# Closing block of a decode kernel: SyncE clears its own six semaphores while its store flies, GpSimd's wait for the store's issue goes

## The chip, the cores and the metric

The kernel runs on one core of a Trainium2 chip. Times are device microseconds of that core. Two lengths must be kept apart. The **span** goes from the first to the last of the kernel's own instructions. The **measured time** is longer: it also holds what runs behind the kernel's last instruction, called the runtime's part here (its semaphore updates go on in the trace of the kernel before from 130.621 to 132.072 us, 1.79 us past the last instruction at 130.283). ("Time less span" below is the plain difference of the two lengths; what lies behind the span's end is 0.29 us more.)

## The reference

One decode step: a query of one token attends to the last 4096 of 32768 cached keys with 32 heads over 16 cached ones, and beside it a dense layer with gelu runs on the same token; a gate mixes the two.

```python
g = _sigmoid((x * gate_w).sum(-1, keepdims=True))
a = _A_ref(x, A_k_cache, A_v_cache, A_wq, A_wo)    # q = x wq; softmax(q k) v; wo
b = _B_ref(x, B_w1, B_b1, B_w2, B_b2)              # gelu(x w1 + b1) w2 + b2
return g * a + (1 - g) * b                         # 1 x 1 x 576, bf16
```

## The kernel before

It streams 53.6 MB of weights and caches and ends with two copies, one store and a closing block:

```python
    out_row = const.tile([1, D], BF16, name="out_row")
    nc.scalar.copy(out=out_row[:, DH:D], in_=y_out[1])
    nc.vector.tensor_copy(out=out_row[:, 0:DH], in_=y_out[0])
    nc.sync.dma_start(out=out.rearrange("a b d -> (a b) d"), in_=out_row[:])
```

The closing block is written by hand over the one that the framework makes. Its semaphores have numbers 99 to 110: 99 is raised by GpSimd's own instructions, 105 by VectorE, 106 by TensorE, 108 by ScalarE, the others by loads, 110 by the store. Number 96 is the gather count of the block.

```python
    def store_ends_program(nc):
        ...
        last = copy.replace(
            leave, sync_info=mybir.SyncInfo(on_wait=[landed], on_update=[taken])
        )
        kept = [arrive, last]          # SyncE: a DRAIN raises the gather count; wait for the landing
        for engine in (
            mybir.EngineType.Activation,
            mybir.EngineType.PE,
            mybir.EngineType.DVE,
        ):                             # one DRAIN each raises the gather count
            kept.append(next(i for i in end.instructions if i.engine == engine))
        ours = [i for i in end.instructions if i.engine == pool]
        others = mybir.SyncInfo(on_wait=waits, on_update=[])
        kept += [copy.replace(ours[0], sync_info=others), ours[1]]   # GpSimd: all waits, then gather >= 4
        reset, clear, spare, spare2 = ours[3:7]
        lo, hi = reset.reset_range_start, reset.reset_range_stop
        for n, (a, b) in enumerate(((lo, sem), (sem + 1, hi))):
            ...                        # GpSimd: DRAIN and range clear of 99..109, then of an empty range
        end.instructions = kept
```

GpSimd may clear only when SyncE has issued the store, since the store's issue waits for the semaphores of VectorE and ScalarE (in the trace of the kernel before they are raised at 129.070 and 129.046 us, the store's issue starts at 129.122, the clears write from 129.903). That is what the gather count of four is for.

## Time and profile before

| | before |
|---|---|
| time, median of runs | 132.34 us (132.31 to 132.40) |
| span | 130.28 us |
| time less span, mean of 11 runs in one set | 1.98 us, single runs scatter by 0.03 |
| last arithmetic ends | 129.06 us |
| store issued / landed | 129.12 / 130.25 us |

How to read it: the page's busy shares say little here, because semaphore instructions are not counted as busy. The prediction below shows the lines that matter: the closing line in the view of one line of code (kind of instruction, count, duration in ns as min/median/max, first and last start), and the waits of SyncE's queue. The records of semaphore updates are in the same trace. The records of single waits in that trace last 17 to 51 ns and do not hold the waiting: SyncE's wait for the landing is one of 17 ns behind 0.6 us without a record. A record of two waits can hold some: GpSimd's on 107/105 lasts 1682 ns.

### The profile page before, as it was taken

What the parts mean: (1) busy time and instruction counts of PE and PEld (TensorE: products, weight loads), DVE (VectorE), ACT (ScalarE), POOL (GpSimd) and SP (SyncE); (2) the same over time, 40 slices, a digit from 0 to 9 for tenths busy, and PEclk for the clock granted to TensorE, in tenths of its full rate; (3) what the DMA queues carried; (4) which work ended last, traced back from release to release, by engine and by line L of the source; (5) the groups of instructions that cost most, each with busy time, mean ns of one, the idle gap of its engine ahead of it and who ended that gap; (6) DMA issues with size and microseconds to landing.
All of it is one profiled execution on the core that took longest, in us unless ns stands there. A gap on an engine that the chain in (4) does not pass through costs nothing.

```text
span 130.3 us, 2411 instructions
## 1 busy us (share of the span) xinstructions
PE 80.7 (62%) x1145; PEld 46.1 (35%) x1077; DVE 53.7 (41%) x49; ACT 8.3 (6%) x18; POOL 10.1 (8%) x34
## 2 busy tenths in 40 slices
PE   0036999476003998949909995985300930899973
PEld 0036949475000121202201121685300920864641
DVE  0056100300079969999999995604000020010001
ACT  3000000003000000030003003021000000000001
POOL 5029930000000000000000000000000000000000
PEclk9999999999999999999996899975555555555999
DMA  7999999899999899899999999899999999999980
GB/s 232 421 436 439 468 401 498 363 463 438 392 448 463 372 453 483 372 443 473 392 433 463 412 412 463 376 444 473 397 423 448 423 407 421 430 427 421 403 354 25
DMA packets 2508, 53.75 MB, mean 413 GB/s; under 512 B 286, under 2 KB 290, under 8 KB 580
## 3 DMA queue, kind: packets, MB, share of 16 engines
q1 hardware_dynamic: 2490, 53.61, 96.5%
q8 instruction: 8, 0.13, 0.4%
q10 hardware_dynamic: 10, 0.01, 0.0%
HBM read 53.62 MB, written 0.00 MB: 412 GB/s over the span
## 4 chain that ended last, share of the span: by engine, by line
DMA 52%; DVE 24%; PE 14%; issue 6%; SPq 2%
DMA k_t<-in_A_k_cache_dram 27%; DMA w_t<-in_B_w_dram 25%; DVE kt L494 19%; PE s_ps L516 7%; PE o_ps L603 5%; DVE m L532 3%; DVE pt L565 2%; PE y_ps L359 1%; SPq L651 1%; DVE mr L535 1%; SPq L658 0%; SPq L194 0%; PE mt_ps L541 0%; DVE out_row L702 0%; SPq L190 0%
## 5 line engine op out<-in xcount | busy, mean ns | idle before, releaser
L516 PE MATMUL s_ps<-kt,qz_flat 128*128 128x512 bf16 x128 | 32.6, 412 | 17.2 <-DVE kt L494 10.4
L494 DVE STREAM_TRANSPOSE kt<-k_t 128x4096 f32<-128x4096 f32 x8 | 35.3, 4432 | 11.7 <-DMA k_t<-in_A_k_cache_dram 10.3
L603 PE MATMUL o_ps<-pt,v_t 128*128 128x8 bf16 x512 | 14.2, 167 | 16.8 <-DMA v_t<-in_A_v_cache_dram 14.8
L516 PEld LDWEIGHTS <-qz_flat 128*128 128x128 bf16 x64 | 6.8, 107 | 40.3 <-issue 40.2
L603 PEld LDWEIGHTS <-v_t 128*128 128x128 bf16 x512 | 14.1, 102 | 17.5 <-DMA v_t<-in_A_v_cache_dram 15.1
L387 PEld LDWEIGHTS <-w_t 128*128 128x128 bf16 x162 | 10.2, 165 | 0.9 <-issue 0.9
L387 PE MATMUL h_ps<-x,w_t 128*128 128x2 bf16 x162 | 10.4, 202 | 0.0
L359 PE MATMUL y_ps<-w_t,gt 128*1 128x288 bf16 x72 | 7.2, 363 | 1.2 <-DMA w_t<-in_B_w_dram 1.2
L553 ACT ACTIVATE p_t<-s_ps,negm 128x1024 bf16<-128x1024 f32 x4 | 4.5, 1113 | 50.9 <-DVE negm L549 50.9
L633 DVE RECIPROCAL rg<-mt_ps 128x32 f32<-128x32 f32 x1 | 0.4, 358 | 15.5 <-PE mt_ps L628 15.5
L565 DVE STREAM_TRANSPOSE pt<-p_t 128x1024 bf16<-128x1024 bf16 x4 | 4.9, 1224 | 2.7 <-ACT p_t L553 2.7
L425 PE MATMUL q_ps<-x,wq_t 128*128 128x2 bf16 x144 | 4.0, 166 | 2.7 <-DMA wq_t<-in_A_wq_dram 2.7
L702 DVE CAST out_row<-y_ps 1x288 bf16<-1x288 f32 x1 | 0.4, 445 | 11.7 <-PE y_ps L359 11.7
L308 PE MATMUL xs_ps<-one_b,rows 1*128 1x1 bf16 x9 | 0.7, 195 | 7.4 <-DVE rows L302 7.4
L532 DVE TENSOR_REDUCE m<-s_ps 128x1 f32<-128x1024 f32 x4 | 4.8, 1196 | 1.1 <-PE s_ps L516 1.1
L359 PEld LDWEIGHTS <-gt 128*1 128x1 bf16 x72 | 3.7, 99 | 3.6 <-issue 1.6
L425 PEld LDWEIGHTS <-wq_t 128*128 128x128 bf16 x144 | 3.9, 104 | 2.8 <-DMA wq_t<-in_A_wq_dram 2.8
L396 DVE COPY hacc<-h_ps 128x36 f32<-128x36 f32 x1 | 0.2, 196 | 10.6 <-PE h_ps L387 10.6
L359 PE MATMUL y_ps<-wo_t,ov 128*1 128x288 bf16 x62 | 4.3, 286 | 0.2 <-DMA wo_t<-in_A_wo_dram 0.2
L661 DVE TENSOR_TENSOR om<-o_ps,rgh 128x128 bf16<-128x128 f32 x1 | 0.3, 292 | 8.8 <-PE o_ps L603 8.8
L302 DVE COPY rows<-rows 1x1152 bf16<-1x1152 bf16 x1 | 0.7, 748 | 6.5 <-DMA rows<-in_A_x_dram 6.5
L359 PEld LDWEIGHTS <-ov 128*1 128x1 bf16 x62 | 2.6, 83 | 1.8 <-issue 0.8
(77 smaller groups left out, 39.1 us busy)
## 6 DMA issues: line engine op xcount, KB each, us to landing
k_t<-in_A_k_cache_dram SPq DMA_DIRECT2D x4, 4096.0 KB, 31.8
v_t<-in_A_v_cache_dram SPq DMA_DIRECT2D x4, 4096.0 KB, 23.2
wq_t<-in_A_wq_dram SPq DMA_DIRECT2D x1, 4608.0 KB, 25.8
w_t<-in_B_w_dram SPq DMA_DIRECT2D x1, 2880.0 KB, 14.2
w_t<-in_B_w_dram SPq DMA_DIRECT2D x1, 2592.0 KB, 23.1
w_t<-in_B_w_dram SPq DMA_DIRECT2D x1, 2304.0 KB, 8.1
wo_t<-in_A_wo_dram SPq DMA_DIRECT2D x1, 2304.0 KB
wo_t<-in_A_wo_dram SPq DMA_DIRECT2D x1, 2160.0 KB
```

What stands on the lines that cost most here:

```text
L302: nc.vector.tensor_copy(out=xdup.rearrange("p (d t) -> p d t", t=2), in_=x_row.rearrange("p (d o) -> p d o", o=1).to_broadcast([1, D, 2]),)
L359: last = nc.tensor.matmul(y_out[s], lhsT=vec, rhs=row[:, s * DH : (s + 1) * DH], start=start, stop=stop, skip_group_check=True,)
L387: nc.tensor.matmul(h_ps[:, j:NF:NJ], lhsT=w1_t[:, i, j:FH:NJ], rhs=x2[:, i, :], start=False, stop=(i == NI - 1 and j == NJ - 1), skip_grou ...
L425: nc.tensor.matmul(q_ps[:, j : Hq : Hq // 2], lhsT=wq_t[:, i, j * Dh : (j + 1) * Dh], rhs=x2[:, i, :], start=(i == 0 and j == 0), stop=(i ...
L494: lambda: nc.vector.transpose(out=kt[g, f][:].bitcast(FP32), in_=keys.rearrange("p c d -> p (c d)").bitcast(FP32),),
L516: last = nc.tensor.matmul(s_ps[g][:, u * 512 : (u + 1) * 512].rearrange("p (c k) -> p c k", k=32), lhsT=qz(g, j, 2 * f + half), rhs=kv[:, ...
L532: queue("dve", lambda: nc.vector.reduce_max(out=m1[:], in_=s_ps[g][:], axis=AX.X))
L535: lambda: nc.vector.tensor_scalar(out=mr[:], in0=hi16[:], scalar1=m1[:, 0:1], scalar2=None, op0=ALU.mult),
L553: nc.scalar.activation(out=p_t[:].rearrange("p c k -> p (c k)"), in_=s_ps[g][:], func=ACT.Exp, bias=negm[:, 0:1], scale=SCALE, accum_out=s ...
L565: lambda: nc.vector.transpose(out=pt[:, g, :, :].rearrange("p c q -> p (c q)"), in_=p_t[:].rearrange("p c k -> p (c k)"),),
L603: last = nc.tensor.matmul(o_ps[:, 8 * g : 8 * g + 8, 0], lhsT=v_t[g][:, c, :], rhs=pt[:, g, c % 32, 8 * (c // 32) : 8 * (c // 32) + 8], st ...
L651: nc.sync.dma_start(out=wo_t[:, r0:r1, :].rearrange("p r n -> p (r n)"), in_=wo_src[:, 0 : 4 * RW, :].rearrange("h (a r) n -> h a (r n)", ...
```

## The change

The intent: GpSimd shall not wait for the store's issue. For that, the semaphores that SyncE still needs are no longer GpSimd's to clear; SyncE subtracts them itself, one instruction each, while the store flies.

```diff
-        landed = next(w for w in waits if w.id == sem)
-        waits.remove(landed)
-        last = copy.replace(
-            leave, sync_info=mybir.SyncInfo(on_wait=[landed], on_update=[taken])
-        )
-        kept = [arrive, last]
+        first = min(w.id for w in store.sync_info.on_wait)
+        mine = [w for w in waits if w.id >= first and w.id != sem]
+        # ... and TensorE's total, and last the store's own semaphore
+        waits = [w for w in waits if w.id < first]
+        kept = []
+        for w, name in zip(mine, names):
+            # taken: "sem-sub-imm" of w.wait_value
+            kept.append(copy.replace(leave, name=name,
+                sync_info=mybir.SyncInfo(on_wait=[w], on_update=[taken])))
...
-        kept += [copy.replace(ours[0], sync_info=others), ours[1]]
+        three = mybir.SyncInfo(
+            on_wait=[copy.replace(came.on_wait[0], wait_value=3)],
+            on_update=[copy.replace(came.on_update[0], update_value=3)],
+        )
+        kept += [copy.replace(ours[0], sync_info=others), copy.replace(ours[1], sync_info=three)]
-        for n, (a, b) in enumerate(((lo, sem), (sem + 1, hi))):
+        for n, (a, b) in enumerate(((lo, first), (stop, hi))):
```

As built: SyncE has six semaphore instructions (108, 105, 107, 109, 106, 110 in this order) and no DRAIN; GpSimd waits for three, has two waits fewer (those on 107/105 and 109/108), and clears 99 to 104.

More of the change, by code (lines that the diff above doesn't have):

```diff
@@ L119, in store_ends_program @@
         sem = store.sync_info.on_update[0].id
+        act = mybir.EngineType.Activation
+        names = [i.name for i in end.instructions if i.engine == sp]
+        names += [i.name for i in end.instructions if i.engine == act][1:]
         drain, arrive, leave = [i for i in end.instructions if i.engine == sp][:3]
         waits = list(drain.sync_info.on_wait)
-        landed = next(w for w in waits if w.id == sem)
-        waits.remove(landed)
-        taken = mybir.SyncUpdate(
-            sync_type="semaphore",
-            id=sem,
-            ant_name=landed.ant_name,
-            update_mode="sem-sub-imm",
-            update_value=landed.wait_value,
-            update_reg=None,
-        )
@@ L132, in store_ends_program @@
-        last = copy.replace(
-            leave, sync_info=mybir.SyncInfo(on_wait=[landed], on_update=[taken])
-        )
-        kept = [arrive, last]
+        pe = [
+            u
+            for i in body.instructions
+            if i.engine == mybir.EngineType.PE and i.sync_info
+            for u in i.sync_info.on_update
+        ]
+        first = min(w.id for w in store.sync_info.on_wait)
+        mine = [w for w in waits if w.id >= first and w.id != sem]
+        mine.append(
+            copy.replace(
+                mine[0],
+                id=pe[0].id,
+                ant_name=pe[0].ant_name,
+                wait_value=sum(u.update_value for u in pe),
+            )
+        )
@@ new lines, in store_ends_program @@
+        mine.append(next(w for w in waits if w.id == sem))
+        stop = max(w.id for w in mine) + 1
+        assert sorted(w.id for w in mine) == list(range(first, stop))
+        waits = [w for w in waits if w.id < first]
+        own = [i for i in body.instructions if i.engine == sp and i.sync_info]
+        last_wait = max(
+            n for n, i in enumerate(own) if any(w.id < first for w in i.sync_info.on_wait)
+        )
+        last_load = max(
+            n for n, i in enumerate(own) if any(u.id < first for u in i.sync_info.on_update)
+        )
@@ new lines, in store_ends_program @@
+        assert last_wait <= last_load
+        assert len(names) >= len(mine)
+        kept = []
+        for w, name in zip(mine, names):
+            taken = mybir.SyncUpdate(
+                sync_type="semaphore",
+                id=w.id,
+                ant_name=w.ant_name,
+                update_mode="sem-sub-imm",
+                update_value=w.wait_value,
+                update_reg=None,
+            )
+            kept.append(
+                copy.replace(
+                    leave,
+                    name=name,
+                    sync_info=mybir.SyncInfo(on_wait=[w], on_update=[taken]),
+                )
+            )
@@ L143, in store_ends_program @@
         others = mybir.SyncInfo(on_wait=waits, on_update=[])
-        kept += [copy.replace(ours[0], sync_info=others), ours[1]]
+        came = ours[1].sync_info
+        three = mybir.SyncInfo(
+            on_wait=[copy.replace(came.on_wait[0], wait_value=3)],
+            on_update=[copy.replace(came.on_update[0], update_value=3)],
+        )
+        kept += [copy.replace(ours[0], sync_info=others), copy.replace(ours[1], sync_info=three)]
         reset, clear, spare, spare2 = ours[3:7]
         lo, hi = reset.reset_range_start, reset.reset_range_stop
-        for n, (a, b) in enumerate(((lo, sem), (sem + 1, hi))):
+        for n, (a, b) in enumerate(((lo, first), (stop, hi))):
             raw = list(clear.instr)
```

## The prediction

To read it: in the trace of the kernel before, semaphore 2 is raised nine times, five blocks of semaphores are written, and semaphore 2 is raised nine times again. The author takes each nine raises for a barrier of the five engines, a "serpentine" (through the engines and back).

> **What bounds the kernel now.** I read the page first, then the timeline of the last microsecond, then the view of the closing block's line with the waits of SyncE's queue, and last the trace's own list of semaphore updates, because the closing block hardly shows anywhere else. The page:
>
> ```profile
> span 130.3 us, 2411 instructions
> DMA 52%; DVE 24%; PE 14%; issue 6%; SPq 2%
> ```
>
> For most of the span the loads set the pace; the change touches none of that. The timeline from 127 us on:
>
> ```profile
> start us, us, engine line op out<-in xcount [idle before <-releaser]
> 128.62 0.45 DVE L702 CAST out_row<-y_ps 1x288 bf16<-1x288 f32 x1 [11.72 <-PE y_ps L359]
> 128.65 0.39 ACT L701 CAST out_row<-y_ps 1x288 bf16<-1x288 f32 x1 [11.56 <-PE y_ps L359]
> 129.12 0.28 SPq L703 DMA_DIRECT2D out_dram<-out_row  x1
> ```
>
> The last arithmetic ends at 129.06 us, the store's issue runs from 129.12 to 129.40, and yet the span ends at 130.28 and the measured time is 132.34. So 3 us of the measured time lie behind the last computation, and 2 us of them behind the span. The change acts only there. Its line (L729 of the old kernel) in the view of one line, where the columns are duration in ns (min/median/max) and first and last start:
>
> ```profile
> L729 POOLq EVENT_SEMAPHORE  x6: 17/43/1682, 116.8 to 129.7; - x6
> L729 POOLq DRAIN  x3: 26/51/77, 129.2 to 130.0; - x3
> L729 POOLq EVENT_SEMAPHORE_RANGE_CLEAR  x2: 33/64/95, 129.9 to 130.1; - x2
> L729 PEldq DRAIN  x1: 543/543/543, 128.1 to 128.1; - x1
> L729 DVEq DRAIN  x1: 477/477/477, 128.6 to 128.6; - x1
> L729 ACTq DRAIN  x1: 419/419/419, 128.7 to 128.7; - x1
> L729 SPq DRAIN  x1: 207/207/207, 129.5 to 129.5; - x1
> L729 SPq EVENT_SEMAPHORE  x1: 17/17/17, 130.3 to 130.3; - x1
> ```
>
> And the waits of SyncE's queue:
>
> ```profile
> SPq L703 <- DVE out_row L702: 27.6, 1, 27.6
> SPq L729 <- SPq L729: 0.6, 1, 0.6
> ```
>
> The reader is to see two tails. SyncE: store issued, a DRAIN of 207 ns that raises the gather count, then 0.6 us of waiting for the store to land, then one semaphore instruction of 17 ns. GpSimd: waits for the other engines, then DRAIN, clear, DRAIN, clear. The records with all digits, with the semaphore updates of the same trace (numbers as built: 96 gather, 110 the store's, 2 not the kernel's):
>
> ```
> 128.671 129.081 129.116 129.671  sem 96 raised by PE, ACT, DVE, SyncE
> 129.562 130.249                  sem 110 raised (store issued; store landed)
> 129.696-129.713                  GpSimd's wait for four on sem 96
> 130.061-130.094                  GpSimd's second range clear, its last instruction
> 130.266-130.283                  SyncE's wait for the landing, its last instruction
> 128.903 129.231 130.621 130.666 130.689 130.786 130.826 130.860 130.906   sem 2
> 131.715 131.749 131.787 131.831 131.855 131.953 131.991 132.026 132.072   sem 2
> ```
>
> [...] semaphore 2 is raised nine times, resets of five blocks of about 51 follow (7-53, 54-104, 105-155, 156-206, 207-255, 130.82 to 131.63 us), then nine again, 357 ns from first to last. [...]
>
> **Who gates the end.** In the second serpentine nothing is late, and its hops are 34, 38, 44, 24, 98, 38, 35, 46 ns. In the first, hops 4 to 9 are 45, 23, 97, 40, 34, 46: ordinary. So the third arrival, at 130.621, is the late one, and the fourth and fifth engines were already waiting. Which engine is third? The blocks of the reset carry a signature: GpSimd's own clear inside the kernel writes groups of four, 21.7 ns apart (129.903, 129.925, 129.946); block 105-155, the third, is written in groups of four 21.8 ns apart, the others at 30, 17.5, 24 and 6.6 ns. So I take the third for GpSimd, the first for PE (the only one done before 128.903), the last for SyncE. GpSimd's last instruction ends at 130.094, 0.19 us before SyncE's, but it needs 130.621 - 130.094 = 0.527 us to arrive; PE needed 128.903 - 128.658 = 0.245 and ACT at most 129.231 - 129.072 = 0.159. **So GpSimd, whose end looks earlier in the span, sets the end of the program.**
>
> **The change part by part.**
> - *GpSimd's wait.* It now waits for three (PE, ACT, DVE): the last raise is at 129.116 instead of 129.671, 0.555 us earlier. The two double waits on semaphores now SyncE's (107/105 and 109/108) go, so it stands at the gather wait long before. The steps after it are the same five: old spacing from the end of that wait to the end of the last clear is 130.094 - 129.713 = 0.381 us. With the old reaction of 129.713 - 129.671 = 0.042: 129.116 + 0.042 + 0.381 = 129.54. Arrival at the barrier with the same 0.527: 130.07, before 130.62.
> - *SyncE.* Its DRAIN of 207 ns goes; five waits with a subtraction come, all already satisfied, before the sixth, which waits for the landing as before. The one such record on SyncE in the opening (0.716, next instruction 0.794) gives 78 ns apiece: 5 x 78 = 0.39 us, from 129.46 to 129.85. The landing is at 130.249: hidden with 0.40 us to spare. The last instruction still ends at 130.283, so **the span hardly moves** (130.28).
> - *The barrier.* Its fifth arrival becomes SyncE's own: 130.283 plus its tail x. The trace only bounds x: SyncE arrived no later than its turn, so x is under 130.689 - 130.283 = 0.406. The tails seen are 0.159 and 0.245 on two engines and 0.527 on GpSimd. I choose x = 0.22, near the first two, as an estimate: arrival at 130.50 in place of 130.689, **0.19 us saved**. Everything behind (four hops, resets, second barrier) moves with it unchanged.
> - *Sum:* 132.34 - 0.19 = 132.15 us. Of GpSimd's 0.555 us, two thirds are not paid out, because the store's flight takes over as the bound.
>
> **The rivals.**
> 1. *SyncE's tail is as long as GpSimd's was allowed to hide, x near 0.38.* Then only 0.02 us is saved: 132.32. For it: GpSimd's tail of 0.527 shows that tails differ. Against it: PE and ACT.
> 2. *The third arrival is SyncE's (130.283 + 0.338), not GpSimd's.* Then the change takes away what was hidden anyway: 132.34. Against it: the signature of the reset, and that block 207-255 would have to be another's.
> 3. *The five subtractions cost far more than 78 ns, or hold the store up.* They'd have to cost 0.16 us each to reach the landing; at 0.25 each the end would be 0.4 us later, 132.5 at most with what is saved. Against it: SyncE's records of this kind last 17 to 28 ns.
> 4. *A short x, 0.12:* 0.29 us saved, 132.05; the next floor is GpSimd at 130.07, with SyncE's turn at 130.13, out of reach.
>
> **Range and chances.** The first steps (GpSimd free, SyncE hidden) I hold at 8 in 10 or more; the size hangs on x alone, between 0.12 and 0.4. Rivals 1 and 2 set the upper end at 132.34, rival 4 the lower, with some hundredths for the spread of runs (132.33 to 132.40 before): 132.02 to 132.34. Two per cent are 2.6 us; all that lies behind the last computation is 3 us, and most of it is the runtime's or the store's. Hence 0.99 for within 2% and 0.005 on each side.
>
> **What would show it right or wrong.** Right: no DRAIN on SyncE in the closing line, six semaphore instructions on it, five between 129.4 and 130.0 and one near 130.3; GpSimd's clears near 129.3 and 129.5; a span of 130.3 as before; a third raise of semaphore 2 near 130.07 and the fifth near 130.5, with a gap before the fifth and not the third. The third still near 130.6 would mean that it isn't GpSimd's or that its 0.527 us is no constant; the sixth SyncE instruction well after 130.3 would mean that the subtractions or the store's flight grew; the fifth near 130.69 would mean rival 1. A time change without a shift of these marks would be noise.

The forecast's sum: 132.34 - 0.19 = 132.15 us, the 0.19 from 130.689 (the fifth raise), 130.283 (SyncE's end) and the estimate x = 0.22. The "17 to 28 ns" of rival 3 leave out two of SyncE's records in that trace, of 363 and 27544 ns.

## The result, and the profile after

The changed kernel takes 131.76 us (median; 131.71 to 131.95), the kernel before 132.34 in the same rounds. The ratio is 0.9959, with a 95% interval of 0.9941 to 0.9976. Ratios here are the mean time of one kernel's runs over that of the other's of the same rounds, so not quite the ratio of the medians. The change is within 2%, as predicted, but the gain is 0.58 us by the medians in place of 0.19, and the median lies below the predicted range.

The page of the changed kernel, first line and the chain's shares by engine:

```profile
span 130.3 us, 2413 instructions
DMA 52%; DVE 24%; PE 13%; issue 6%; SPq 2%
```

Span and chain are as before: whatever was gained was gained behind the span. The timeline of the last microseconds:

```profile
128.62 0.45 DVE L742 CAST out_row<-y_ps 1x288 bf16<-1x288 f32 x1 [11.72 <-PE y_ps L399]
129.13 0.28 SPq L743 DMA_DIRECT2D out_dram<-out_row  x1
```

The closing line, and the wait of SyncE's queue in it:

```profile
L769 SPq EVENT_SEMAPHORE  x6: 17/17/17, 129.5 to 130.3; - x6
L769 POOLq EVENT_SEMAPHORE  x4: 17/30/43, 116.7 to 129.1; - x4
L769 POOLq DRAIN  x3: 31/41/64, 125.4 to 129.4; - x3
L769 POOLq EVENT_SEMAPHORE_RANGE_CLEAR  x2: 33/52/71, 129.3 to 129.5; - x2
```

```profile
SPq L769 <- SPq L769: 0.5, 1, 0.5
```

GpSimd's clears start at 129.3 and 129.5, where they started at 129.9 and 130.1. SyncE's DRAIN is gone, its six instructions stand between 129.5 and 130.3, and its last wait in front of the landing has shrunk only from 0.6 to 0.5 us, since five short instructions now fill the rest. With all digits, from the trace's records:

```
                                        before     changed
GpSimd: gather wait ends                129.713    129.163
GpSimd: last instruction ends           130.094    129.517
SyncE: five subtractions                   -       129.466 to 129.791
store landed                            130.249    130.255
SyncE: last instruction ends            130.283    130.289
first closing barrier, raise 3          130.621    130.044
                       raise 5          130.689    130.426
                       raise 6          130.786    130.470
                       raise 9          130.906    130.589
second closing barrier, last raise      132.072    131.740
end of the measured time (clock record) 132.57     132.03
  behind the last raise                   0.499      0.293
```

So the 0.54 us by which these two profiled runs differ (132.28 and 131.74) come in steps: 0.263 us at the fifth raise, 0.317 at the ninth, 0.332 at the last raise, and then 0.206 us more behind the last raise. The first part is what the prediction was about. The last part it did not know of. Over all runs that last part is a little smaller: time less span fell from 1.98 to 1.47 us (9 runs of the changed kernel), and 0.33 of these 0.51 are at the last raise, which leaves 0.18.

### The profile page after: what moved, and what is told of

Same layout as the page of the kernel before. It is cut to its first block, busy times and chain, and to the rows that moved or that the text cites. A ratio compares the mean times of both kernels' runs of the same rounds, so it can differ in the third digit from the quotient of the medians.

```text
span 130.3 us, 2413 instructions
## 1 busy us (share of the span) xinstructions
PE 80.3 (62%) x1145; PEld 45.9 (35%) x1077; DVE 53.7 (41%) x49; ACT 8.3 (6%) x18; POOL 10.1 (8%) x34
## 4 chain that ended last, share of the span: by engine, by line
DMA 52%; DVE 24%; PE 13%; issue 6%; SPq 2%
DMA k_t<-in_A_k_cache_dram 27%; DMA w_t<-in_B_w_dram 25%; DVE kt L534 19%; PE s_ps L556 7%; PE o_ps L643 5%; DVE m L572 3%; DVE pt L605 2%; SPq L698 1%; PE y_ps L399 1%; SPq L691 1%; DVE mr L575 1%; PE mt_ps L581 0%; DVE out_row L742 0%; SPq L234 0%; SPq L230 0%
## 5 line engine op out<-in xcount | busy, mean ns | idle before, releaser
L348 PEld LDWEIGHTS <-rows 1*128 1x128 bf16 x9 | 0.6, 152 | 7.4 <-DVE rows L342 7.4
```

## The experiments

Theory 1: GpSimd's arrival, 0.527 us behind its last instruction, held up the first closing barrier; freed of its wait it no longer does, and SyncE's landing wait takes over. Rival A: the gain came from SyncE's side, its missing DRAIN or its own clearing. For the 0.2 us behind the last raise theories came up on the way: chance or the shift itself (V), and the length of an engine's instruction stream (L).

A barrier here is nine raises of semaphore 2; in the second barrier they took 0.357 us from first to last in the trace before and 0.372 in the changed kernel's. The author reads them as five arrivals, of TensorE, ScalarE, GpSimd, VectorE and SyncE, and four on the way back in reverse order. The experiments bear this out for three engines: edits on GpSimd alone moved raise 3 (a_noempty by 0.133 us, a_pool3 by 0.17) and, in the second barrier, raise 7 (a_pool3, by 0.23), edits on SyncE raise 5 (a_sp4, by 0.222), edits on VectorE raises 4 and 6 (a_dve6, a_dve2). For the rest it was not shown. Between the two barriers the five blocks of semaphores are written, the reset: 0.79 us together in the changed kernel, of 1.31 us from the fifth raise to the last.

All marks in the table are us behind the store's issue in the profiled run, which removes the scatter of the loads (the issue itself came anywhere from 128.80 to 129.35 us). "GpSimd/VectorE" are the profiled instructions on these engines. "Time less span" is the mean over all runs of the kernel in its rounds, with the scatter of single runs in brackets; the listed spans are rounded to 0.1 us. What an edit adds to SyncE's end lies inside the span and does not show in this column (a_sp4).

| kernel | GpSimd/VectorE | raise 3 | raise 5 | raise 9 | last raise | end behind it | median us | ratio to before (95%) | time less span |
|---|---|---|---|---|---|---|---|---|---|
| before | 60/59 | 1.499 | 1.567 | 1.784 | 2.950 | 0.499 | 132.34 | | 1.98 (0.03) |
| b_same | 60/59 | 1.498 | 1.565 | 1.782 | 2.935 | 0.489 | 132.22 | 0.9997 (0.9984 to 1.0009) | 1.97 (0.03) |
| changed | 58/59 | 0.916 | 1.298 | 1.461 | 2.612 | 0.293 | 131.76 | 0.9959 (0.9941 to 0.9976) | 1.50 (0.17) |
| a_same | 58/59 | 0.912 | 1.303 | 1.466 | 2.618 | 0.318 | 131.72 | 0.9958 (0.9946 to 0.9970) | 1.44 (0.15) |
| a_gather4 | 58/59 | 1.462 | 1.529 | 1.747 | 2.900 | 0.292 | 132.11 | 0.9986 (0.9973 to 0.9999) | 1.77 (0.06) |
| b_noempty | 58/59 | 1.385 | 1.452 | 1.670 | 2.819 | 0.413 | 131.97 | 0.9978 (0.9966 to 0.9991) | 1.76 (0.09) |
| a_nosub | 58/59 | 0.918 | 1.320 | 1.483 | 2.648 | 0.266 | 131.84 | 0.9962 (0.9949 to 0.9975) | 1.59 (0.11) |
| a_pool3 | 61/59 | 1.085 | 1.300 | 1.463 | 2.860 | 0.202 | 131.94 | 0.9966 (0.9954 to 0.9978) | 1.62 (0.05) |
| a_pool9 | 67/59 | 1.804 | 1.872 | 2.088 | 3.252 | 0.381 | 132.58 | 1.0016 (1.0004 to 1.0028) | 2.17 (0.05) |
| a_sp4 | 58/59 | 0.906 | 1.520 | 1.683 | 2.847 | 0.416 | 132.00 | 0.9973 (0.9961 to 0.9985) | 1.48 (0.13) |
| a_pad2 | 60/59 | 0.910 | 1.310 | 1.474 | 2.625 | 0.500 | 132.03 | 0.9981 (0.9967 to 0.9994) | 1.64 (0.02) |
| a_pad1 | 59/59 | 0.912 | 1.299 | 1.462 | 2.604 | 0.337 | 131.97 | 0.9975 (0.9962 to 0.9987) | 1.61 (0.09) |
| b_move2 | 58/61 | 1.503 | 1.569 | 2.208 | 3.355 | 0.119 | 132.35 | 1.0004 (0.9992 to 1.0017) | 2.03 (0.02) |
| a_noempty | 56/59 | 0.783 | 1.304 | 1.467 | 2.611 | 0.297 | 131.83 | 0.9964 (0.9951 to 0.9976) | 1.52 (0.14) |
| b_fewer2 | 58/59 | 1.508 | 1.575 | 1.793 | 2.936 | 0.118 | 132.13 | 0.9983 (0.9971 to 0.9995) | 1.77 (0.13) |
| b_pad2 | 62/59 | 1.498 | 1.565 | 1.783 | 2.926 | 0.485 | 132.06 | 0.9983 (0.9968 to 0.9998) | 1.82 (0.15) |
| a_dve1 | 58/60 | 0.907 | 1.300 | 1.464 | 2.739 | 0.303 | 131.90 | 0.9968 (0.9956 to 0.9980) | 1.56 (0.05) |
| a_dve2 | 58/61 | 0.916 | 1.310 | 1.629 | 2.776 | 0.119 | 131.65 | 0.9957 (0.9945 to 0.9969) | 1.45 (0.02) |
| a_dve4 | 58/63 | 0.917 | 1.310 | 1.473 | 2.618 | 0.120 | 131.68 | 0.9951 (0.9938 to 0.9964) | 1.26 (0.02) |
| a_dve6 | 58/65 | 0.907 | 1.297 | 1.461 | 2.602 | 0.119 | 131.63 | 0.9950 (0.9937 to 0.9962) | 1.27 (0.05) |

### The two kernels once more: a_same, b_same

No edit. Expected:

> The changed kernel once more, to see its spread and a second trace. Theory 1 (GpSimd's late arrival held up the closing barrier; now SyncE's own arrival does): third raise of semaphore 2 near 130.04 us, fifth near 130.43, ninth near 130.59, time 131.7 to 131.95. The measured end fits, in the two traces at hand, the end of a last instruction fetch counted from GpSimd's first memset (132.271 and 131.739 us against 132.28 and 131.74). Theory F1: that fetch has a length that varies from run to run (0.34 to 0.55 us), so the time scatters by 0.2 us with all barrier marks in place. Theory F2: the length belongs to the kernel, and the fetch is again 0.34 us.

> The kernel before once more. All theories: time 132.3 to 132.4, third raise of semaphore 2 at 130.62. F1 (the last fetch varies from run to run): its length anywhere from 0.3 to 0.55 us and a time down to 132.1 now and then. F2 (the length belongs to the kernel): 0.53 us again.

The barrier marks repeat within 0.02 us in both. Time less span scatters by 0.03 us in the kernel before and by 0.15 in the changed one. The last instruction fetch in the trace (a DMA record of the kind "instruction", 8192 bytes; the eight inside the kernel have 16384 each) lasted 0.531 and 0.418 us in the two traces of before, 0.342 and 0.380 in the two of the changed kernel, so its length is not the kernel's own (F1, not F2). In the changed kernel the measured time ended with that fetch both times; in b_same the fetch ended 0.347 us behind the last raise and the time nonetheless at 0.489. The kernel before therefore ends with something else, which the records do not name, 0.489 and 0.499 us behind the last raise in its two traces. F1 is not the whole account either: it would scatter the times of both kernels by 0.2 us, and only the changed one scatters so. No record shows anything that waits for what lies behind the last raise; it counts because the measured time runs to the end of the clock record.

### Undo GpSimd's earlier start: a_gather4

```diff
-        kept = []
-        for w, name in zip(mine, names):
+        kept = [arrive]
+        for w, name in zip(mine, [n for n in names if n != arrive.name]):
...
-            on_wait=[copy.replace(came.on_wait[0], wait_value=3)],
-            on_update=[copy.replace(came.on_update[0], update_value=3)],
+            on_wait=[copy.replace(came.on_wait[0], wait_value=4)],
+            on_update=[copy.replace(came.on_update[0], update_value=4)],
```

> The changed kernel with one part undone: SyncE raises the gather count again with its DRAIN behind the store, and GpSimd waits for four; SyncE still takes its six semaphores back itself. Theory 1: GpSimd's last instruction back near 130.1, third raise near 130.62, time 132.3, all of the gain lost. Rival A (the gain came from SyncE's side, its own clearing or the shorter range that GpSimd clears): time stays at 131.8.

Its closing line in the view of one line of code:

```profile
L769 SPq EVENT_SEMAPHORE  x6: 17/17/17, 129.7 to 130.2; - x6
...
L769 POOLq EVENT_SEMAPHORE_RANGE_CLEAR  x2: 33/52/71, 129.8 to 129.9; - x2
...
L769 SPq DRAIN  x1: 207/207/207, 129.4 to 129.4; - x1
```

SyncE still does all its own clearing, but GpSimd's clears are late again, and with them the third raise (1.462 us) and the ninth (1.747; the kernel before has 1.784). The edit brings SyncE's DRAIN back too, but SyncE's last instruction ends at 1.153 us (1.161 without the DRAIN), so the DRAIN holds nothing up. Rival A is out: of the 0.32 us at the ninth raise, 0.28 go with GpSimd's wait; the other 0.04 are what GpSimd's last instruction still ends earlier than in the kernel before (0.934 in place of 0.972 us), with its shorter clear (71 ns in place of 95). But the expectation that all of the gain would be lost missed: the time is 132.11 and not 132.3; the end behind the last raise stayed short (0.292). That was the first sign of the second part.

### Take a cost off GpSimd alone, in both kernels: b_noempty, a_noempty

```diff
-        for n, (a, b) in enumerate(((lo, sem), (sem + 1, hi))):
+        for n, (a, b) in enumerate(((lo, sem),)):
```

and in the changed kernel `((lo, first), (stop, hi))` becomes `((lo, first),)`.

> The kernel before without GpSimd's second DRAIN and range clear, whose range is empty. SyncE is untouched. Theory 1: GpSimd ends 0.117 us earlier (129.98 in place of 130.094), the third raise comes at 130.50 and the barrier ends 0.117 us earlier: 132.22, or somewhat less or more by the last fetch. Rival: SyncE's landing wait (130.283) gates already: 132.34 as before.

> The changed kernel without GpSimd's second DRAIN and range clear, which are empty (56 instructions on GpSimd). Theory 1: GpSimd has room now, so the fifth raise stays 1.30 us behind the store's issue and the time at 131.75; in the kernel before, the same cut moved the barrier by 0.114 us. Theory L: the end behind the last raise as in the changed kernel or shorter, not longer.

Before the change, GpSimd's last instruction ends 0.120 us sooner (0.972 to 0.852), and that gives 0.114 us at the third raise and the same at the ninth (1.784 to 1.670): GpSimd gates. After the change GpSimd comes 0.13 us sooner (0.916 to 0.783) and the fifth raise doesn't move: it no longer gates. In b_noempty the time fell by more than the 0.117 expected (0.22 less in time less span): again GpSimd's stream was shorter by two.

### Is SyncE's clearing hidden, and does SyncE gate: a_nosub, a_sp4

```diff
-        for w, name in zip(mine, names):
+        for w, name in zip(mine[-1:], names):
```

```diff
+        again = mybir.SyncInfo(on_wait=arrive.sync_info.on_wait, on_update=[])
+        kept += [copy.replace(leave, name=f"I-{9000 + n}", sync_info=again) for n in range(4)]
```

(a_sp4, behind SyncE's six instructions; the wait is for a semaphore to be zero, which it is by then.)

> The changed kernel with SyncE taking back only the store's semaphore; the other five are left to the reset that the runtime does behind the kernel. Theory 1: the five subtractions (0.39 us) lie wholly under the store's flight, so SyncE's last instruction stays at 130.29, the fifth raise at 130.43 and the time at 131.75. Rival 3 of the prediction (they hold something up): 0.1 to 0.4 us faster. F2 (code length sets the last fetch): the fetch changes its length by some 0.2 us although the barrier marks stay.

> The changed kernel with four more waits on SyncE, already satisfied, behind its landing wait; 0.073 us each, 0.29 us. Theory 1: SyncE gates, without room, so the fifth raise moves from 130.43 to 130.72 and the time from 131.75 to 132.05. If GpSimd or another engine gated: less than that or nothing.

Without the five subtractions SyncE's last instruction ends 1.173 us behind the store's issue, with them at 1.161 and 1.165: they cost nothing. (That the other five semaphores are left to the runtime's reset made no result wrong.) Four more waits behind the landing, expected to take 0.29 us (the five subtractions start 0.067 to 0.089 us apart in the changed kernel's trace), move SyncE's end by 0.233 us and the fifth, ninth and last raise by 0.222 to 0.235: SyncE gates the changed kernel, without room.

### How much room GpSimd has: a_pool3, a_pool9

```diff
+        again = mybir.SyncInfo(on_wait=[waits[0]], on_update=[])
+        kept += [copy.replace(ours[1], name=f"I-{9000 + n}", sync_info=again) for n in range(3)]
```

(behind GpSimd's gather wait; a_pool9 has nine.)

> The changed kernel with three more waits on GpSimd, already satisfied, between its gather wait and its clears; about 0.07 us each, 0.2 us in all. Theory 1: GpSimd has 0.31 us to spare (third raise 130.04, SyncE's turn at 130.43 less two hops of 0.068), so the third raise moves to 130.25, the fifth stays at 130.43 and the time at 131.75. If GpSimd still gated: 131.95.

> The same with nine such waits, 0.63 us. Theory 1: the room of 0.31 us is used up; GpSimd's third raise comes near 130.67 and gates again, the fifth follows it by 0.068 and the sixth by 0.097 more: time near 132.3 to 132.4, as in the kernel before. If only SyncE counted: 131.75.

Three waits moved the third raise by 0.17 us and the fifth not at all, as expected. Nine made GpSimd gate again, as expected, but by more than was put in: its last instruction ended 0.54 us later, and then it took 0.878 us to arrive in place of 0.527. With three, GpSimd's turn on the way back in the second barrier came 0.270 us after VectorE's in place of 0.038. So a stall of 0.23 us (a_pool3) and one of 0.35 us (a_pool9) turned up at two places of the runtime's part. That it wanders there as GpSimd's stream grows is a guess; b_pad2 below does not fit it.

### Stream length on GpSimd: a_pad2, a_pad1, b_fewer2, b_pad2, b_move2

```diff
+        again = mybir.SyncInfo(on_wait=[next(w for w in waits if w.id == 99)], on_update=[])
+        kept += [copy.replace(ours[1], name=f"I-{9000 + n}", sync_info=again) for n in range(2)]
```

(a_pad2 and b_pad2, ahead of GpSimd's waits, satisfied long before; a_pad1 has one.)

```diff
+        waits = [w for w in waits if w.id not in (101, 102, 103)]
```

(b_fewer2: the waits on three load semaphores go, which stood in two instructions.)

```diff
-    nc.gpsimd.memset(one_b[:], 1.0)
+    nc.vector.memset(one_b[:], 1.0)
-    nc.gpsimd.memset(om_t[:], 0.0)
+    nc.vector.memset(om_t[:], 0.0)
```

(b_move2.)

> The changed kernel with two more waits on GpSimd ahead of its gather wait, satisfied since 17 us, so no barrier mark should move; GpSimd's stream is as long again as in the kernel before (60 profiled instructions in place of 58). So far the time less the span is 1.98 us in the kernel before (spread of single runs 0.03), 1.44 to 1.50 in the changed one (spread 0.15), but the ninth raise of the first barrier accounts for only 0.32 of it; the rest lies between the last raise of semaphore 2 and the end of the measured time (0.49 us in the kernel before, 0.29 in the changed one). Theory L (the change makes GpSimd's stream two instructions shorter, and that moves something the runtime does behind the barrier): the end is 0.49 us behind the last raise again, time less span 1.65, time near 131.95 with the small spread of before. Theory V (chance, or the shift itself): as the changed kernel, 1.47 and 131.75.

> The same with one more wait (59 instructions). Theory L: either as with two or as with none, the same in all runs. Theory V: 131.75.

> The kernel before with two small memsets (one_b, om_t) moved from GpSimd to VectorE, so that GpSimd's stream is two instructions shorter (58), as in the changed kernel; the closing block is that of the kernel before. Barrier marks as before: third raise 1.50 us behind the store's issue, ninth 1.78. Theory L: the end comes 0.1 to 0.2 us sooner behind the last raise, time less span 1.80 in place of 1.98, time near 132.15. Theory V: 1.98 and 132.3.

> The kernel before without two of GpSimd's waits (on three load semaphores that others have waited for by then), so that GpSimd has 58 profiled instructions and no other engine's stream changes; nothing on the path to its gather wait goes. Theory L (GpSimd's stream length decides what comes behind the barrier): ninth raise 1.78 us behind the store's issue as before, end 0.3 us behind the last raise in place of 0.49, time less span 1.80 in place of 1.97 with a larger spread, time near 132.1. If the length doesn't matter: 1.97.

> The kernel before with two more idle waits on GpSimd ahead of its gather wait (62). Theory L, from the run with 61 instructions, where GpSimd's second pass of the second barrier took 0.27 us in place of 0.04: the stall lies inside the second barrier again, its last raise is 0.2 us or more late, and the end no earlier than before: time less span 1.95 to 2.2. If the length doesn't matter: 1.97 and the second barrier's hops as before.

a_pad2 came out as theory L had it, to the hundredth: the barrier marks stay within 0.013 us, the end is 0.500 us behind the last raise as in the kernel before, time less span is 1.64 with the small scatter of before (0.02). b_fewer2 is the mirror image: marks as before, time less span down from 1.98 to 1.77, scatter up to 0.13. (Its profiled run, with the end at 0.118, is the shortest of its six: 1.57, one more at 1.63, the rest 1.83 to 1.90.) So in both kernels two idle instructions on GpSimd, nowhere on the path, are worth some 0.2 us of measured time (0.18 and 0.21 on average): of these two lengths 60 is the worse and 58 the better. a_pad1 lies between, from 1.48 to 1.68; theory L had expected all its runs to be alike.

b_pad2 missed its expectation: 62 instructions did not stall inside the second barrier as 61 had, and its time less span (1.82) is below that of 60. So these idle instructions matter, but no simple rule for the length came out, and what runs at the end of the 60-instruction kernels is not in the records. Why they matter stays open.

b_move2 missed too (time less span 2.03 where theory L had 1.80), and for a reason that led further: it had made VectorE's stream longer, and VectorE's turn in the first barrier (raise 6) came 0.520 us after SyncE's, in place of 0.097.

### Stream length on VectorE: a_dve1, a_dve2, a_dve4, a_dve6

```diff
             kept.append(next(i for i in end.instructions if i.engine == engine))
+        still = mybir.SyncInfo(on_wait=arrive.sync_info.on_wait, on_update=[])
+        there = copy.replace(leave, engine=mybir.EngineType.DVE, sync_info=still)
+        kept += [copy.replace(there, name=f"I-{9000 + n}") for n in range(2)]
```

(1, 2, 4 or 6 idle waits behind VectorE's DRAIN.)

> The changed kernel with two idle waits on VectorE behind its DRAIN (61 instructions; VectorE is ready 1 us before its turn, so nothing waits for them). Theory L for VectorE: a stall of 0.4 us between the fifth and the sixth raise of the first barrier, as in the run with the moved memsets: sixth raise 1.75 us or more behind the store's issue in place of 1.34. The end behind the last raise may shrink. Time 131.9 to 132.2. If VectorE's length doesn't matter: 131.75.

> The same with one idle wait on VectorE (60). Theory L: either the stall inside the barrier, as with two, or none, as with the changed kernel; the place of the boundary is not known. If there is none and the end is no later: 131.75.

> The changed kernel with four idle waits on VectorE behind its DRAIN. If the stall sits at a fixed place of VectorE's stream: it falls ahead of VectorE's fourth raise or just behind it, while SyncE waits for the store, so it is hidden: fifth raise 1.30, sixth 1.34 us behind the store's issue as in the changed kernel, last raise at 2.61, the last fetch over before that, end 0.12 us behind it: time less span 1.28, time near 131.55, small spread. If the fetch is another engine's: 1.47 and 131.75.

> The same with six, as a check that the place needn't be hit exactly: VectorE ends its own part 1.2 us before its turn, six waits take some 0.4 us, the stall 0.2 to 0.45. Same expectation: time less span 1.28, time near 131.55. If it comes too late for its turn: fifth raise later than 1.30 and no gain.

With six, the stall can be seen plainly. Four answers of the view of the closing line for VectorE, cut to successive windows:

```profile
L772 DVEq EVENT_SEMAPHORE  x2: 21/21/21, 129.3 to 129.3; - x2
...
L772 DVEq EVENT_SEMAPHORE  x2: 21/21/21, 129.4 to 129.5; - x2
...
L772 DVEq EVENT_SEMAPHORE  x1: 21/21/21, 129.9 to 129.9; - x1
...
L772 DVEq EVENT_SEMAPHORE  x1: 21/21/21, 130.0 to 130.0; - x1
```

The six equal waits start 0.071, 0.139, 0.207, 0.276, 0.757 and 0.833 us behind the store's issue: 0.068 us apart, and once 0.481. Nothing in the program distinguishes the fifth from the fourth, so the 0.41 us belong to a place of the stream. The rest follows from where that place falls:

```
idle waits on VectorE                      0      1      2      4      6
start of its block in the reset          1.904  2.035  1.652  1.489  1.476
raise 6 behind raise 5                   0.044  0.044  0.200  0.043  0.044
last instruction fetch starts            2.563  2.492  2.114  1.433  1.431
end of the time behind the last raise    0.293  0.303  0.119  0.120  0.119
```

With none, VectorE's reset starts 0.56 us after its raise (1.342 to 1.904); with six, 0.135 us (1.341 to 1.476): the stall has left that place. With two it falls, in part, between the fifth and the sixth raise. (The expectation had it there whole, with the sixth raise at 1.75 us or later and a time of 131.9 to 132.2; measured were 1.510 and 131.65, so this run missed.) With four or six it falls while VectorE waits for SyncE anyway, and is hidden. The last fetch moves with VectorE's stream and not with GpSimd's (2.563 in the changed kernel, 2.577 in a_pad2, 2.550 in a_pool3), so most likely it is VectorE's. Once it is over before the last raise, the time ends 0.12 us behind that raise: in a_dve2, a_dve4, a_dve6 and in b_move2. It ends there also in b_fewer2, whose trace has no such fetch although its VectorE stream is that of the kernel before; and a_pool9 has two such fetches. Neither is explained. That the stall itself is a wait for instructions is not shown: no record says what VectorE waits for there.

In a_dve1 VectorE's reset came 0.13 us later, and with it VectorE's turn in the second barrier: neither branch of its expectation (a stall inside the barrier as with two, or none).

**A version with a shorter end than both:** the changed kernel with four or six idle waits on VectorE took 131.68 and 131.63 us. Time less span, the measure without the loads' scatter, is 1.26 over their 11 runs and 1.47 over the 9 runs of the changed kernel, a difference of 0.20 with an interval of about 0.1 to 0.3 (from the scatter of the single runs). That is the 1.28 that was expected; the times came out 0.1 us above the expected 131.55. By the times alone, whose intervals overlap, they would not be told apart from the changed kernel.

## Why the prediction was wrong

**What bounds the end: right.** That GpSimd, though its last instruction ends before SyncE's, gates the first barrier through its tail of 0.527 us was borne out by b_noempty (0.120 us taken off it, 0.114 us gained at the barrier) and a_gather4. The tail was 0.527 to 0.528 again in the changed kernel. The tails differ by engine: 0.126 to 0.147 us for SyncE where it gates, at most 0.16 for ScalarE if raise 2 is its.

**GpSimd's part: right.** Predicted end of its last instruction 129.54 and arrival 130.07; measured 129.517 and 130.044.

**SyncE's subtractions hidden: right.** Predicted from 129.46 to 129.85, measured 129.466 to 129.791; the span stayed at 130.29.

**The tail x of SyncE: right in kind, wrong in size.** The estimate was 0.22 us; it is 0.137. That is 0.08 us more gain, so the fifth raise came 0.263 us earlier in place of 0.19. It was still within the band of 0.12 to 0.4 that the prediction gave it.

**"Everything behind (four hops, resets, second barrier) moves with it unchanged": wrong, in two places.** The hop from the fifth to the sixth raise shrank from 0.097 to 0.044 us, where VectorE had made its fourth raise 0.338 us before the fifth in place of 0.023: 0.05 us. The slow hop of 0.098 in the undisturbed second barrier, which the prediction took for ordinary, goes with VectorE coming straight from its own raise: in the first barriers it was 0.096 to 0.098 where the fifth raise followed the fourth by 0.023 or 0.024 us, and 0.043 to 0.045 where it followed by 0.17 us or more, except in the two runs with VectorE's stall at that place (a_dve2, b_move2). And the end of the measured time is not tied to the last raise: it lay 0.499 us behind it and then 0.293, which is 0.206 us. This second place is the step that put the result out of the range. The prediction had listed the two waits that GpSimd loses and counted them as time before the gather wait, where they are worth nothing; a_pad2 shows that giving GpSimd back two idle instructions takes this gain away again, and b_fewer2 that taking two away gains as much in the kernel before. Why two instructions there do this stays open.

The sum in the profiled runs: 0.186 predicted, 0.077 by x, 0.054 by the hop, 0.015 from the ninth raise to the last (the first raise of the second barrier came 0.78 to 0.81 us behind the ninth in all traces, whatever the kernel), 0.206 behind the last raise; together the 0.54 measured. Up to the last raise alone (0.33 us) the time would have been 132.01, at the lower edge of the range; the sentence that the size "hangs on x alone" made the range too narrow.

One sum of its opening is off as well: it set the measured time of 132.34 against marks of the span and found 3 us behind the last computation and 2 us behind the span. Since the measured time starts at 0.29 us, it is 3.5 and 2.3 us. The forecast of the time does not rest on it.

**The rivals.** Rivals 1 (a long x) and 2 (the third arrival is SyncE's) and 3 (dear subtractions) are refuted by the fifth raise at 130.43, by the third raise that followed GpSimd, and by a_nosub. Rival 4 (x of 0.12) was close.

## What to carry to other kernels

Where the measured time goes on behind the kernel, look at what the barrier there waits for: the engine with the latest last instruction need not be the one that holds it up (in the kernel before SyncE's ended at 130.283 us and GpSimd's at 130.094, but GpSimd's raise came at 130.621 and the barrier with it), and an engine's slack can be read by putting a known delay on it. At a few tenths of a microsecond, moving, adding or dropping an instruction on an idle engine was not neutral here: on VectorE it shifted a stall of about 0.41 us (a_dve6) that sits at a place of the stream, and on GpSimd it changed the end by some 0.2 us. So a control with the same instruction count is needed before such a gain is put down to the edit's idea. On VectorE, which waits anyway, four or six idle waits pushed the stall to where it cost nothing (time less span 1.26 us in place of 1.47).
